# One transfer in place of two for q and k of a pair of heads, with eight tokens in sequence on a partition

## The chip, the cores and the metric

The kernel runs on one core of a Trainium2 chip. The metric is the time of the whole program on the device, in microseconds (us); lower is better.

## The reference, cut to what matters

Three blocks follow one another: an attention over 4 x 8 heads with 576 tokens of 64 values each, a two-layer expert block, and a second block whose two first products are multiplied with each other. The change lies in the loading of the attention's q and k:

```python
Sd = S // factor                      # factor = 4, S = 576
q_d = q.reshape(B, H, Sd, factor, D).mean(axis=3)
k_d = k.reshape(B, H, Sd, factor, D).mean(axis=3)
...
out_d = sm_attn(q_d, k_d, v_d)        # attention among the 144 group means
out_up = np.repeat(out_d, factor, axis=2)
mask = np.abs(pos[:, None] - pos[None, :]) < factor
...                                   # attention within the band |i - j| < 4
return (out_up + out_local).astype(np.float32)
...
h = x @ w_in
g = h * (1.0 / (1.0 + np.exp(-1.702 * h)))
x = g @ w_out
a = x @ w1
b = x @ w2
h = a * b @ w3
out = h @ w_out2
```

All of it is float32. The kernel splits each operand of a large product into a high and a low part and adds three matmuls (`mm3`, lines 118 to 120).

## The kernel before, in words

Heads are worked on in 16 pairs, numbered n = 4 b + hp: four pairs for each of the four batches b. A pair fills 128 partitions after its transposition: 64 values of one head, 64 of the other.

For a pair, `att_load` fetches q and k into the tiles s_q and s_k, one buffer each, and v into s_v. `t_piece` ("T") turns q and k over, so that the 64 values of each head lie on partitions and the 576 tokens along the free dimension (qT, kT, with 144 groups u of 4 tokens r), and adds up the tokens of each group (qd, kd). `s_local` and `s_pool` ("S") form the scores, `p_piece` ("P") transposes the exponentials, `v_pool` and `v_local` ("V") multiply them with v and store x_d.

Pairs 0 to 7 (the first two batches; `PE_T = 2`) are turned over by TensorE: the tile has 72 partitions, each holds 2 times 4 tokens of both heads, and each of two pieces c = 0 and 1 makes four 72 x 128 transposes into a PSUM tile ps_t (line 284), which ScalarE then writes out in group order (line 285). Pairs 8 to 15 take another branch (lines 243 and 280), with 32 x 32 transposes on VectorE.

The transfers of pairs 0 to 7 are issued in line 250, two for q and two for k: on the SyncE queue for pair 0, on ScalarE's own queue for pairs 1 to 7. ScalarE carries these issues out in its own order of instructions, between its activations. Pair n + 2 is loaded in the first `p_piece` of pair n, when pair n + 1 has been turned over; pair 5 is loaded in `s_pool` of pair 4; pair 1 before the loop over the w34 steps.

The pieces of batch 0 are put one by one between the matmuls of the first stage (the product w3 w_out2, tiles ps_w, w3t, w34s), those of later batches between the matmuls of `h_step` and `y_step` for the batch before. The weights come packed in 64-bit words and are decoded on the way: a transfer into `st`, ScalarE's `size_of` (line 166), VectorE's three steps (lines 173, 176, 179), and `split` (lines 114 and 115). Staging tiles come from pools of two and three buffers.

The Tile framework's scheduler makes the order of instructions on every engine when the program is built. It works with priorities and with times that it estimates itself for each instruction and transfer, and gives out buffers in that order. The trace shows this order: pieces of the source stand apart or between one another.

Of the kernel before, what the change touches and what calls it, by code (L numbers as in the profile page):

```python
# [8 lines left out]
F32 = mybir.dt.float32  # L9
# [3 lines left out]
AF = mybir.ActivationFunctionType  # L13
# [7 lines left out]
def fused_kernel(ctx, tc, q, k, v, w_in, w_out1, w1, w2, w3, w_out2, out):  # L21
    nc = tc.nc
    B, H, S, D = q.shape
    FAC = 4
# [9 lines left out]
    UC = SD // 2  # L34
# [37 lines left out]
    att = att_end.enter_context(tc.tile_pool(name="att", bufs=1))  # L72
# [11 lines left out]
    ident = const.tile([128, 128], F32, name="ident")  # L84
# [144 lines left out]
    def head_ap(src, b, hp, tok, dims):  # L229
        off = ((b * H + 2 * hp) * S + tok) * D  # L230
        return bass.AP(src.tensor, src.offset + off, dims)

    def att_load(n, names="qkv", queue=None):
        b, hp = divmod(n, HP)
        queue = queue or nc.scalar
        for name, src in (("q", q), ("k", k)):
            if name not in names:
                continue
            if b >= PE_T:

                st = att.tile([128, S // 32, 32], F32, tag="s" + name, name="s_" + name)
                for i in range(4):
                    nc.sync.dma_start(out=st[i * 32:(i + 1) * 32], in_=bass.AP(
                        src.tensor, src.offset + (b * H + 2 * hp + i // 2) * S * D + i % 2 * 32,
                        [[D, 32], [32 * D, S // 32], [1, 32]]))
                at["s" + name, n] = st
                continue
            st = att.tile([UC, 2, FAC, 2, D], F32, tag="s" + name, name="s_" + name)
            for c in range(2):
                queue.dma_start(out=st[:, c], in_=head_ap(  # L250
                    src, b, hp, c * UC * FAC, [[FAC * D, UC], [D, FAC], [S * D, 2], [1, D]]))
            at["s" + name, n] = st
        if "v" not in names:
            return
        st = att.tile([UC, 2, 2, FAC * D], F32, tag="sv", name="s_v")
        queue.dma_start(out=st, in_=head_ap(
            v, b, hp, 0, [[FAC * D, UC], [S * D, 2], [UC * FAC * D, 2], [1, FAC * D]]))
        at["sv", n] = st
# [15 lines left out]
    def t_piece(n, name, c):  # L274
        if c == 0:
            at[name, n] = att.tile([128, SD, FAC], F32, tag=name + "T", name=name + "T")
        st, dst = at["s" + name, n], at[name, n]
        if n // HP >= PE_T:
            if c == 0:
                nc.vector.transpose(dst.rearrange("p u r -> p (u r)"), st.rearrange("p a b -> p (a b)"))  # L280
        else:
            ps = pst.tile([128, FAC, UC], F32, tag="t", name="ps_t")
            for r in range(FAC):
                nc.tensor.transpose(ps[:, r], st[:, c, r].rearrange("p h d -> p (h d)"), ident[:UC, :UC])
            nc.scalar.activation(dst[:, c * UC:(c + 1) * UC].rearrange("p u r -> p r u"), ps, AF.Copy)
        if c == 1:
            if name == "q":
                d = qd[:, :SD]
            else:
                d = at["kd", n] = att.tile([128, SD], F32, tag="kd", name="kd")  # L290
            if n // HP in QK_V:
                nc.vector.tensor_reduce(d, dst, op=ALU.add, axis=X)
            else:
                nc.gpsimd.tensor_tensor(d, dst[:, :, 0], dst[:, :, 1], op=ALU.add)
                for r in range(2, FAC):
                    nc.gpsimd.tensor_tensor(d, d, dst[:, :, r], op=ALU.add)

    def v_means(n):
        sv = at.pop(("sv", n))
        nc.gpsimd.tensor_tensor(  # L300
            sv[:, :, :, :2 * D], sv[:, :, :, :2 * D], sv[:, :, :, 2 * D:], op=ALU.add)
        vd = at["vd", n] = att.tile([UC, 2, 2, D], F32, tag="vd", name="vd")
        nc.gpsimd.tensor_tensor(vd, sv[:, :, :, :D], sv[:, :, :, D:2 * D], op=ALU.add)
        if n + 1 < B * HP:
            att_load(n + 1, "v")
# [35 lines left out]
    def s_pool(n, own_exp):  # L341
        if n % HP == 0 and n > 0:
            att_load(n + 1, "qk")
# [39 lines left out]
    def p_piece(n, i0, i1):  # L383
        if i0 % NPH == 0 and i0 // NPH >= (n in LOCAL):
            at["PT", n, i0 // NPH] = att.tile(
                [KW, min(NPH, NPT - i0), 128], F32, tag=f"PT{i0 // NPH}", name="PT")
        i0 = i0 if n not in LOCAL else max(i0, NQB)
        ps = pst.tile([KW, i1 - i0, 128], F32, tag="t", name="ps_pt")
        for i in range(i0, i1):
            if i < NQB:  # L390
                src = at["el", n][:, i]
            else:
                kc, j = divmod(i - NQB, NPB)
                src = at["ep", n][:, j, kc * UC:(kc + 1) * UC]
            nc.tensor.transpose(ps[:, i - i0], src, ident)  # L395
        nc.scalar.activation(at["PT", n, i0 // NPH][:, i0 % NPH:i0 % NPH + i1 - i0], ps, AF.Copy)
        first = i0 == (0 if n not in LOCAL else NQB)
        if first:
            v_means(n)
            if n % HP < HP - 1 and n + 2 < B * HP:  # L400
                att_load(n + 2, "qk")
# [110 lines left out]
    def stage(n, what, own_exp):  # L512
        if what == "T":
            return [lambda name=name, c=c: t_piece(n, name, c) for name in "qk" for c in range(2)]
        if n in LOCAL and what in "SPV":
            if what == "S":
                return [lambda: s_pool(n, False)]
            if what == "P":
                return [lambda: p_piece(n, NPH, NPH + 4), lambda: p_piece(n, NPH + 4, NPT)]
            return [lambda: v_pool(n), lambda: l_out(n, 0, HQ), lambda: l_out(n, HQ, NQB)]  # L520
        if what == "S":
            return [lambda: s_local(n, 0, HQ, own_exp), lambda: s_local(n, HQ, NQB, own_exp), lambda: s_pool(n, own_exp)]
        if what == "P":
            return [lambda i=i: p_piece(n, i, min(i + 4, NPT)) for i in range(0, NPT, 4)]
        return [lambda: v_pool(n), lambda: v_local(n, 0, HQ), lambda: v_local(n, HQ, NQB)]
# [460 lines left out]
```

## Time and profile before

| | |
|---|---|
| Time, median of 3 runs | 893.88 us (893.79 to 894.19) |
| The profiled execution | 894.5 us, of which its span from first to last instruction is 892.7 us |
| TensorE, matmuls | 846.7 us busy (95% of the span) |
| VectorE (DVE) | 602.2 us (67%) |
| ScalarE (ACT) | 388.0 us (43%) |
| GpSimd (POOL) | 146.0 us (16%) |
| Mean granted TensorE clock | 0.988 of full speed |

Busy time doesn't count DMA issues: an engine that issues a transfer looks idle in it. The queues that issue are shown with a q (ACTq, SPq). PEld is TensorE's loading of weights, which overlaps its matmuls.

### The profile page before, as it was taken

The numbers are of one execution on the slowest core, as the hardware profiler recorded it, in microseconds if no ns is written. First come the engines' busy times: TensorE is split into PE (matmuls) and PEld (weight loads), VectorE is DVE, ScalarE is ACT, GpSimd is POOL, SyncE is SP. The second block draws the span as 40 slices with busy tenths as digits, with TensorE's granted clock in tenths as the row PEclk, the third lists the DMA queues.
The fourth block names the chain that finished last, engine by engine and source line by source line (L and its number), as shares of the span: only waits on it lengthen the run. The fifth ranks groups of instructions, "written<-read, shape, count | busy, mean of one in ns | idle before, by whom it ended". The sixth has DMA issues, their size and how long they took to land.

```text
span 892.7 us, 13582 instructions
## 1 busy us (share of the span) xinstructions
PE 846.7 (95%) x5132; PEld 711.7 (80%) x5132; DVE 602.2 (67%) x1061; ACT 388.0 (43%) x750; POOL 146.0 (16%) x153
## 2 busy tenths in 40 slices
PE   5689979889999999999999999999999999999998
PEld 4567757666777777777789988889999899989996
DVE  5997597889999999747658784343556455555551
ACT  4667566567756344455336564342112211232111
POOL 7525241233232322301200000000000000000000
PEclk9799999999999999999999999999999999999999
DMA  8866574566665341543247889302556364645521
GB/s 231 271 207 164 154 234 145 155 164 179 152 188 111 78 128 43 162 98 70 64 137 277 322 305 366 130 1 68 226 186 262 107 247 165 250 140 217 196 83 71
DMA packets 140598, 150.76 MB, mean 169 GB/s; under 512 B 86898, under 2 KB 121460, under 8 KB 136436
## 3 DMA queue, kind: packets, MB, share of 16 engines
q1 hardware_dynamic: 119424, 141.21, 49.0%
q10 hardware_dynamic: 21108, 8.69, 4.3%
q8 instruction: 40, 0.66, 0.3%
q14 instruction: 26, 0.21, 0.1%
HBM read 117.75 MB, written 32.11 MB: 168 GB/s over the span
## 4 chain that ended last, share of the span: by engine, by line
PE 57%; DVE 3%; issue 1%; ACT 1%; DMA 0%; DVEq 0%; ACTq 0%
PE ps_ab L120 7%; PE ps_ab L118 7%; PE ps_ab L119 7%; PE ps_y L118 4%; PE ps_y L119 4%; PE ps_y L120 4%; PE ps_h L118 4%; PE ps_h L119 4%; PE ps_h L120 4%; PE ps_o L119 4%; PE ps_o L120 4%; PE ps_o L118 4%; DVE prod L484 1%; PE ps_pt L395 0%; DVE ql L487 0%
## 5 line engine op out<-in xcount | busy, mean ns | idle before, releaser
L118 PE MATMUL ps_h<-x_t,w 128*128 128x512 f32 (+1 forms) x320 | 122.5, 385 | 3.0 <-DVE w L115 2.6
L118 PE MATMUL ps_y<-gh,w 128*128 128x512 f32 (+1 forms) x320 | 122.0, 382 | 0.7 <-ACT gh L114 0.7
L119 PE MATMUL ps_h<-x_t,w 128*128 128x512 f32 (+1 forms) x320 | 119.0, 372 | 0.6 <-DVE x_t L115 0.6
L119 PE MATMUL ps_y<-gl,w 128*128 128x512 f32 (+1 forms) x320 | 118.5, 370 | 1.0 <-DVE gl L115 1.0
L120 PE MATMUL ps_y<-gh,w 128*128 128x512 f32 (+1 forms) x320 | 118.8, 371 | 0.0
L120 PE MATMUL ps_h<-x_t,w 128*128 128x512 f32 (+1 forms) x320 | 118.6, 371 | 0.0
L120 PE MATMUL ps_ab<-b_t,a_in 128*128 128x384 f32 x336 | 112.5, 335 | 0.0
L118 PE MATMUL ps_ab<-b_t,a_in 128*128 128x384 f32 x336 | 112.5, 335 | 0.0
L119 PE MATMUL ps_ab<-b_t,a_in 128*128 128x384 f32 x336 | 112.4, 334 | 0.0
L115 DVE TENSOR_TENSOR gl<-g_t,gh 128x512 fp32r<-128x512 f32 (+1 forms) x80 | 56.3, 706 | 55.6 <-ACT gh L114 55.1
L624 ACT ACTIVATE g_t<-ps_h 128x512 f32<-128x512 f32 (+1 forms) x80 | 44.1, 552 | 103.7 <-PE ps_h L120 102.6
L118 PEld LDWEIGHTS ps_h<-x_t,w 128*128 128x128 f32 x320 | 60.3, 189 | 17.1 <-DVE w L115 4.4
L114 ACT ACTIVATE abh<-ab 128x384 fp32r<-128x384 f32 x24 | 12.6, 526 | 137.5 <-DVE ab L749 137.5
L118 PEld LDWEIGHTS ps_y<-gh,w 128*128 128x128 f32 x320 | 60.3, 189 | 12.5 <-issue 2.2
L119 PEld LDWEIGHTS ps_h<-x_t,w 128*128 128x128 f32 x320 | 60.7, 190 | 10.5 <-DVE x_t L115 1.6
L120 PEld LDWEIGHTS ps_h<-x_t,w 128*128 128x128 f32 x320 | 60.5, 189 | 10.4 <-issue 0.2
L120 PEld LDWEIGHTS ps_y<-gh,w 128*128 128x128 f32 x320 | 60.3, 189 | 10.3
L119 PEld LDWEIGHTS ps_y<-gl,w 128*128 128x128 f32 x320 | 60.4, 189 | 10.1 <-DVE gl L115 1.3
L179 DVE SCALAR_TENSOR_TENSOR dec<-dec,st 128x512 int32<-128x512 int32 x72 | 61.3, 863 | 7.4 <-ACT dec L166 6.6
L118 PEld LDWEIGHTS ps_ab<-b_t,a_in 128*128 128x128 f32 x336 | 63.1, 188 | 0.9
L119 PEld LDWEIGHTS ps_ab<-b_t,a_in 128*128 128x128 f32 x336 | 63.1, 188 | 0.9
L120 PEld LDWEIGHTS ps_ab<-b_t,a_in 128*128 128x128 f32 x336 | 63.1, 188 | 0.0
(149 smaller groups left out, 1645.4 us busy)
## 6 DMA issues: line engine op xcount, KB each, us to landing
a_in<-a_d SPq DMA_DIRECT2D x24, 1792.0 KB
st<-in_moe_w_dram SPq DMA_DIRECT2D x32, 512.0 KB
a_d<-ap SPq DMA_DIRECT2D x8, 1792.0 KB
st<-in_moe_w_out_dram SPq DMA_DIRECT2D x24, 512.0 KB
st<-in_moe_w_in_dram SPq DMA_DIRECT2D x16, 512.0 KB
yr<-y_d SPq DMA_DIRECT2D x12, 384.0 KB
out_dram<-osb SPq DMA_DIRECT2D x17, 256.0 KB
s_v<-in_v_dram ACTq DMA_DIRECT2D x15, 288.0 KB
```

The source lines that it names most:

```text
L114: nc.scalar.activation(hi, raw, AF.Copy)
L115: lo_eng.tensor_tensor(lo, raw, f32(hi), op=ALU.subtract)
L118: nc.tensor.matmul(ps, ll, rh, start=start, stop=False, skip_group_check=more)
L119: nc.tensor.matmul(ps, lh, rl, start=False, stop=False, skip_group_check=more)
L120: nc.tensor.matmul(ps, lh, rh, start=False, stop=stop, skip_group_check=more)
L179: nc.vector.scalar_tensor_tensor(t, t, 3, st[:, :, 0], op0=ALU.logical_shift_left, op1=ALU.bitwise_or)
L484: (nc.vector if o in DVE_V else nc.gpsimd).tensor_tensor(t, at["vl", n][:, o:o + GT], s[:, o].unsqueeze(2).to_broadcast([128, GT, D]), op= ...
L624: nc.scalar.activation(g[:, :n], ps[:, :n], AF.Gelu_apprx_sigmoid)
```

## The change: what it does

`att_load` makes one transfer for q and one for k of a pair, where there were two each. Before, a partition held tokens 4u to 4u + 3 of the first half of the sequence and the same of the second half; now partition u holds tokens 8u to 8u + 7. The pieces c of `t_piece` still take four tokens of each partition, but these are now the groups 2u + c in place of 72c + u. So line 285 writes groups that lie two apart: neighbouring values in the order of its writing are 8 elements apart in qT and kT (32 bytes), where they were 4 apart (16 bytes). The sizes of tiles and the counts of transposes and activations stay.

```diff
-            st = att.tile([UC, 2, FAC, 2, D], F32, tag="s" + name, name="s_" + name)
-            for c in range(2):
-                queue.dma_start(out=st[:, c], in_=head_ap(
-                    src, b, hp, c * UC * FAC, [[FAC * D, UC], [D, FAC], [S * D, 2], [1, D]]))
+            st = att.tile([UC, 2 * FAC, 2, D], F32, tag="s" + name, name="s_" + name)
+            queue.dma_start(out=st, in_=head_ap(
+                src, b, hp, 0, [[2 * FAC * D, UC], [D, 2 * FAC], [S * D, 2], [1, D]]))
...
-                nc.tensor.transpose(ps[:, r], st[:, c, r].rearrange("p h d -> p (h d)"), ident[:UC, :UC])
-            nc.scalar.activation(dst[:, c * UC:(c + 1) * UC].rearrange("p u r -> p r u"), ps, AF.Copy)
+                nc.tensor.transpose(ps[:, r], st[:, c * FAC + r].rearrange("p h d -> p (h d)"), ident[:UC, :UC])
+            nc.scalar.activation(
+                dst.rearrange("p (u c) r -> p c r u", c=2)[:, c], ps, AF.Copy)
```

## Rows read from the trace of the kernel before

**Rows 1.** Busy time by stretch: us, PE, PEld, DVE, ACT, POOL, PEclk, DMA share, GB/s.

```profile
0.00:223.00 223.00, 185.28 (x1349) 140.74 (x1350) 177.78 (x294) 139.65 (x309) 87.89 (x108) 0.95 0.66 190
223.00:893.00 670.00, 661.43 (x3784) 570.94 (x3783) 424.37 (x768) 248.38 (x443) 58.09 (x46) 1.00 0.50 162
20.00:80.00 60.00, 47.31 (x344) 35.48 (x342) 57.82 (x94) 37.11 (x102) 28.09 (x27) 0.89 0.70 215
```

**Rows 2.** Waits of TensorE, 0 to 223 us: total us, times, longest.

```profile
PE ps_w L573 <- DVE dec L179: 17.1, 5, 9.1
...
PE ps_sp L352 <- POOL kd L296: 3.5, 1, 3.5
...
PE ps_pt L395 <- ACT kT L285: 2.5, 2, 1.7
...
PE ps_pt L395 <- ACT PT L396: 1.8, 2, 1.3
```

**Rows 3.** Issues of transfers by tile and line: ns min/median/max, first and last start.

```profile
L250 ACTq DMA_DIRECT2D s_q<-in_q_dram x14: 805/807/1424, 11.2 to 190.7; - x14
L250 SPq DMA_DIRECT2D s_q<-in_q_dram x2: 792/882/971, 1.7 to 2.7; - x2
...
L243 SPq DMA_DIRECT2D s_q<-in_q_dram x32: 311/446/1356, 216.3 to 418.3; - x32
...
L256 ACTq DMA_DIRECT2D s_v<-in_v_dram x15: 307/308/365, 34.9 to 421.4; - x15
```

**Rows 4.** ScalarE's groups by form: count, busy us, mean ns, idle before.

```profile
L739 ACT ACTIVATE u_t<-ps_ab 128x384 f32<-128x384 f32 x24 | 11.8, 492 | 20.5 <-PE ps_ab L120 20.5
L285 ACT ACTIVATE qT<-ps_t 128x288 f32<-128x288 f32 x16 | 10.3, 711 | 5.6 <-PE ps_t L284 5.6
L413 ACT ACTIVATE od<-ps_vp 128x144 f32<-128x144 f32 x16 | 4.5, 283 | 6.6 <-PE ps_vp L410 4.6 <-DVE xo L507 1.9
```

**Rows 5.** VectorE's reductions by form; line 471 reads every ninth element.

```profile
L337 DVE TENSOR_REDUCE mx<-el 128x5 f32<-128x360 f32 x12 | 6.3, 521 | 0.0
L337 DVE TENSOR_REDUCE mx<-el 128x4 f32<-128x288 f32 x12 | 5.3, 440 | 0.0
...
L471 DVE TENSOR_REDUCE r<-s 128x9 f32<-128x63 f32 x4 | 1.1, 264 | 0.1
```

**Rows 6.** Waits of ScalarE, 0 to 223 us: the one put to these loads.

```profile
ACT PT L396 <- DMA s_k<-in_k_dram: 8.1, 4, 2.9
```

**Rows 7.** Timeline around two groups of issues: start, us, then the instruction.

```profile
43.43 1.65 ACTq L250 DMA_DIRECT2D s_k<-in_k_dram  x2
...
45.13 0.60 ACT L396 ACTIVATE PT<-ps_pt 72x512 f32<-72x512 f32 x1 [2.87 <-DMA s_k<-in_k_dram]
...
46.96 0.66 PE L573 MATMUL ps_w<-ident,dec 128*128 128x128 f32 x4 [0.82 <-DVE dec L179]
...
54.07 0.63 PE L573 MATMUL ps_w<-ident,dec 128*128 128x128 f32 x4 [2.23 <-DVE dec L179]
...
71.29 1.89 ACTq L250 DMA_DIRECT2D s_k<-in_k_dram  x2
...
73.88 0.52 PE L395 MATMUL ps_pt<-ident,ep 128*72 128x128 f32 x3 [0.52 <-ACT PT L396]
```

**Rows 8.** Timeline: issues for pair 0 and pair 5, and pair 5's first transposes.

```profile
3.51 2.42 SPq L250 DMA_DIRECT2D s_k<-in_k_dram  x2
...
130.53 0.81 ACTq L250 DMA_DIRECT2D s_q<-in_q_dram  x1
...
137.12 0.41 PE L284 MATMUL ps_t<-ident,s_q 72*128 72x72 f32 x4
```

**Rows 9.** Stretches of 5 us, columns as in the first group.

```profile
40.00:45.00 5.00, 3.94 (x14) 2.91 (x15) 5.00 (x5) 0.60 (x1) 4.81 (x5) 0.66 0.63 187
...
55.00:60.00 5.00, 5.00 (x54) 4.04 (x51) 4.81 (x8) 2.15 (x5) 1.66 (x2) 0.68 0.85 288
...
85.00:90.00 5.00, 3.97 (x36) 3.03 (x35) 1.73 (x3) 2.40 (x5) 2.67 (x4) 1.00 0.80 215
```

## The prediction, made before the result was known

> **What bounds the kernel now.** I read the busy time by stretch first. TensorE works 661.4 of the last 670 us, so nothing that the change touches can win there; pairs 8 to 15 take their own branch and stay as they are. Up to 223 us, where pairs 0 to 7 are loaded and turned over, TensorE works 185.3 us and stands idle for 37.7 us [rows 1]. A gain or a loss can only come out of these 37.7 us. Next the waits of TensorE in that stretch: 17.1 us end with VectorE's last decoding step in line 179, 9.1 us of them once, before the first weights are there; waits that ScalarE ends are 2.5 us for kT and 1.8 us for PT, and 3.5 us is for GpSimd's sum kd, which stands behind kT [rows 2]. Between 20 and 80 us VectorE is the fullest engine: 57.8 of 60 us [rows 1]. What ScalarE saves there reaches TensorE only as far as VectorE can follow.
>
> **What is removed: half of the issues.** The old transfers number 32: 28 on ScalarE's queue and 4 on SyncE's. An issue on ScalarE takes 0.805 us at 72 partitions with 8 rows of 256 bytes each [rows 3]. After it there are 14 on ScalarE and 2 on SyncE with 16 rows per partition. Rows of 256 bytes stay rows of 256 bytes, because the two heads still lie interleaved in the tile; bytes and rows per pair stay the same (2 x 1,152 rows), so I count no time of the DMA engines as won or lost.
>
> What one larger issue takes isn't in the trace. The nearest rows: v, with 4 rows of 1 KB on each of 72 partitions, 0.307 us; pairs 8 to 15, with 18 rows of 128 bytes on 32 partitions, 0.311 us at the least; q, with 8 rows, 0.805 us [rows 3]. The second has as many rows as q in all (576), so the number of rows alone doesn't explain 0.805. If what costs is the four-level pattern, the issue stays at 0.805 us, and ScalarE gets back 14 x 0.805 = 11.3 us. If it grows with the rows of a partition, the slope from v to q is (0.805 - 0.307) / 4 = 0.125 us a row, 16 rows take 1.80 us, and against 2 x 0.805 = 1.61 us this loses 14 x 0.19 = 2.7 us. I take 1.2 us, in the middle, since the rows point both ways: 14 x (1.61 - 1.2) = 5.7 us of ScalarE's time.
>
> **How much of that is on the path?** An issue that stands between two activations hides behind the one still running. Where two or four stand in a row ScalarE waits: 8.1 us in four places are put to the issues for s_k [rows 6]. I followed the two where TensorE waits soon after. From 41.7 to 45.1 us all four issues of pair 2 run; PT is copied only at 45.13, after 2.87 us, decoding comes behind it, and TensorE waits 0.82 us at 46.96. But the next wait for line 179, 2.23 us at 54.07 [rows 7], stands behind a VectorE without a gap, which then simply waits longer: I count 0 there, at most 0.8. At 71.29 us the two issues for s_k hold back PT, and TensorE waits 0.52 us at 73.88 [rows 7]. One issue in place of two shortens 1.61 to 1.2 us, thus takes some 0.4 us off it. In the other two places TensorE has matmuls at hand: 0. Sum: -0.4 us; with a flat 0.805 us and both places in full 0.8 + 0.5 = -1.3 us; with 1.80 us some +0.2 us.
>
> **SyncE at the start.** The two issues for k last until 5.93 us [rows 8]; the loads of weights behind them in SyncE's queue come up to 2 us earlier if an issue stays flat. The first two weight tiles were issued ahead, and the first wait of 9.1 us is for these. I count 0.
>
> **Waiting for a whole transfer.** The first piece now needs all 8 tokens of a partition. The tightest case before is pair 5: the second issue for q starts at 130.53 us and ends at 131.34, the first transpose comes at 137.12 [rows 8], 5.8 us later and without a wait. The new transfer is issued in the first one's place, sooner than that. I count 0; work that covers it are the matmuls in between. With that cover gone it would cost the difference of the landings, below 0.8 us (one issue) for a pair.
>
> **The other order of writing.** Line 285 writes 288 values per partition in 0.711 us. Activations with values side by side: 144 in 0.283 and 384 in 0.492 us, that is 0.871 ns a value, and 0.408 us for 288 [rows 4]. So the 16-byte step costs 0.30 us already. For 32 bytes there is no row of ScalarE. The nearest is a reduction on VectorE that reads 36 bytes apart: its neighbours give (521 - 440) / 72 = 1.125 ns a value and 116 ns beside, thus the 63 values take (264 - 116) / 63 = 2.35 ns each, 2.1 times as long [rows 5]; ScalarE's 16-byte step stands at 1.92 against 0.871 ns, 2.2 times. The wider step thus seems to cost nothing more: bounds 0 and another 0.30 us on each of 32 writes, 9.7 us of ScalarE. I take 0. The Trainium skill (SBUF — State Buffer, section Door 1: The DMA port swizzle) says that an access which goes on to a new 16-byte line pays. By that rule the 16-byte step pays for every value already and 32 bytes change nothing: 0 us by the rule, 0 by the row taken, and no run here shows the wider step.
>
> The Trainium skill (DMA: Bandwidth & Descriptors, section Rules for kernel authors) tells one to put small transfers together, as under 64 KB they are mostly overhead. These have 144 KB, and the trace shows no wait for their landing; by its 2.0 us for each transfer (same page, Anatomy of one DMA) 16 fewer would be an estimated 32 us, all beside other work.
>
> **The order made anew.** The scheduler makes the order from its own estimates, and 16 instructions fewer will shift pieces up to 223 us. How much this moves I bound from rows: in 40 to 45 and 55 to 60 us the granted clock is 0.66 and 0.68, that is, partly at the lower of two levels, 1.2 in place of 2.4 GHz. With TensorE at work throughout the second, such a stretch costs (1 - 0.68) x 5 = 1.6 us. A stretch with gaps, such as 85 to 90 us, leaves 1.0 us idle, and the next after it was granted less [rows 9]. So one such event more or less is worth 1.6 to 2.6 us, more than all that the issues give.
>
> **Rivals, each with its time.** My sum starts from the profiled execution, 894.5 us (892.7 of span and 1.8 around it), which is 0.6 above the median of 893.88; differences are applied to the median. A measurement tells 0.2%, 1.8 us, from no change.
> - No change that can be told (0.38): -0.4 us, rounded for the small chance of more to -0.6: 893.3 us. Its own range is 892.1 to 895.6.
> - ScalarE's freed time reaches TensorE (0.20): 0.8 + 0.5 us, and another 0.8 where VectorE's decoding at 54.07 moves up as well: -2.1, 891.8 us. For it speaks that line 179 ends most of TensorE's waits [rows 2], against it a full VectorE [rows 1]. It decides if an issue stays below 0.9 us and VectorE shows gaps at 45 us.
> - The new order loses or spares a stretch at the lower clock: faster by 1.6 and the 0.4, 891.9 us (0.16); slower by 1.6 + 1.0 us, 896.5 us (0.18). The slower one decides if one more idle time of about a microsecond falls between 25 and 150 us with a lower clock behind it.
> - The wider step costs (0.08): from 0.85 us for line 285. At 1.0 us kT is late twice (two activations each) in the waits of 2.5 us for kT and once in the 3.5 us for kd [rows 2]: 3 x 2 x 0.30 = 1.8, and 0.6 for the first pair: +2.4, 896.3 us.
> - That the change doesn't do what it says, at 1.61 us or more for an issue, gives 893.9 to 894.1 us and lies in the first case.
>
> Faster by over 0.2%: 0.20 + 0.16 = 0.36; within: 0.38; slower: 0.18 + 0.08 = 0.26. The range that leaves out no more than 2 in 10 runs from 890.2 (the faster cases with 1.6 us more) to 896.9 us.
>
> **What would show it.** In the trace after: issues of line 250, 14 on ScalarE, at about 1.2 us (0.8 or 1.8 at the bounds); line 285 at 0.71 us; the wait of ScalarE put to the loads of k at half of 8.1 us or less; idle time of TensorE up to 223 us at 37 us, with the same kinds of waits; after 223 us nothing. The prediction is wrong if that idle time moves by over 2 us, if the stretches at the lower clock are more or fewer, or if line 285 passes 0.85 us.

## The result, and the profile after

The changed kernel takes 905.49 us (median of 4 runs, 903.11 to 907.36) against 893.84 (891.24 to 894.19) of the kernel before: a ratio of 1.0136, with a 95% interval of 1.0099 to 1.0172. It is slower by 11.6 us. The profiled execution took 905.09 us, 903.3 of them its span. Lines behind the transfer stand one higher in this kernel: 249 for the transfer, 283 for the transposes, 284 for the write.

First the edits themselves. The issues of transfers of the changed kernel (columns as in [rows 3]) and the group of ScalarE that answers to line 285 in [rows 4]:

```profile
L249 ACTq DMA_DIRECT2D s_q<-in_q_dram x7: 807/829/1429, 11.1 to 195.5; - x7
L249 SPq DMA_DIRECT2D s_q<-in_q_dram x1: 976/976/976, 1.6 to 1.6; - x1
L249 ACTq DMA_DIRECT2D s_k<-in_k_dram x7: 807/807/830, 14.2 to 197.5; - x7
L249 SPq DMA_DIRECT2D s_k<-in_k_dram x1: 1722/1722/1722, 2.7 to 2.7; - x1
```

```profile
L284 ACT ACTIVATE qT<-ps_t 128x288 f32<-128x288 f32 x16 | 11.7, 758 | 9.2 <-PE ps_t L283 9.1
```

Half as many issues, and on ScalarE's queue each as short as before: 0.807 us with 16 rows to a partition as with 8. (On SyncE's queue the one issue for k took 1.722 us; the two for k took 2.42 us together [rows 8].) The write grew from 0.711 to 0.758 us. ScalarE's wait of 8.1 us put to the loads of k [rows 6] is gone. Each part of the edit thus costs little or gives something back, and still 11.6 us are lost. Busy time by stretch (columns as in [rows 1]):

```profile
0.00:223.00 223.00, 181.08 (x1315) 138.13 (x1315) 170.67 (x287) 136.38 (x300) 82.19 (x102) 0.92 0.65 186
223.00:893.00 670.00, 662.95 (x3793) 571.73 (x3792) 431.60 (x773) 255.12 (x451) 65.14 (x51) 1.00 0.50 162
```

Behind 223 us little changed; ahead of it TensorE worked 4.2 us less in the same time, at a granted clock of 0.92 in place of 0.95. Where the loss arises can be seen by milestones. At 84 us both kernels are in step: the fourth copy of w34s (line 586) begins at 84.00 us before and at 84.04 after. Pair 3's local scores (line 333) come at 101.30 and 104.30; the first product of y (`ps_y`) begins at 140.37 us before and at 150.85 after, and the first u_t of the second block (line 739) at 615.94 and 626.55. So the loss, 10.5 us, arises between 84 and 151 us and is only carried on behind that. The waits of TensorE from 84 to 156 us, of the kernel before and then of the changed one (us in total, times, longest):

```profile
PE ps_sp L352 <- POOL kd L296: 3.5, 1, 3.5
PE ps_t L284 <- DVE xo L426: 1.7, 1, 1.7
PE ps_pt L395 <- POOL el L375: 1.2, 1, 1.2
PE ps_h L119 <- DVE x_t L115: 0.6, 1, 0.6
```

```profile
PE ps_h L118 <- ACT x_t L114: 4.8, 1, 4.8
PE ps_pt L395 <- POOL el L375: 4.3, 1, 4.3
PE ps_t L283 <- DVE xo L426: 2.5, 1, 2.5
PE ps_h L119 <- DVE x_t L115: 2.2, 1, 2.2
PE ps_sp L352 <- DVE el L336: 0.3, 1, 0.3
```

In sum these are 7.0 us before and 14.1 after, 7.1 more. The clock adds to it. Stretches of 5 us of the changed kernel: us, TensorE's busy time, granted clock, DMA share, GB/s:

```profile
135.00:140.00 5.00, 0.64 (x1) 0.89 0.99 262
140.00:145.00 5.00, 2.80 (x10) 0.50 0.85 256
145.00:150.00 5.00, 4.71 (x61) 0.92 0.70 247
```

After 4.4 us of idle time TensorE goes on at a granted clock of 0.50, the lower of its two levels (1.2 in place of 2.4 GHz); in the next stretch, where it works 4.71 of 5 us, it is granted 0.92. Over 84 to 156 us the mean granted clock is 0.95 before and 0.88 after. On TensorE's 57.6 us of work there that is about 57.6 x (1 - 0.88 / 0.95) = 4.2 us, an estimate from these two rows (before, then after; columns as in the last ones), though the two stretches don't hold quite the same work; 7.1 + 4.2 = 11.3 us stand against 10.5 seen.

```profile
84.00:156.00 72.00, 64.34 (x472) 0.95 0.63 183
84.00:156.00 72.00, 57.60 (x434) 0.88 0.61 175
```

None of the five waits is for the loads of q and k or for line 284, which were changed. What stands ahead of them is seen in the timeline of the changed kernel around batch 0's last pair (pair 3), the lines that matter of each engine:

```profile
114.19 0.43 DVE L173 TENSOR_SCALAR st<-st 128x512 int32<-128x512 int32 x1 [1.88 <-DMA st<-in_moe_w_out_dram]
...
117.00 0.43 DVE L173 TENSOR_SCALAR st<-st 128x512 int32<-128x512 int32 x1 [0.84 <-DMA st<-in_moe_w_in_dram]
...
118.02 0.22 DVE L372 RECIPROCAL sm<-sm 128x12 f32<-128x12 f32 x1
...
118.12 1.78 POOL L300 TENSOR_TENSOR s_v<-s_v 72x512 f32<-72x512 f32 x1 [7.66 <-DMA s_v<-in_v_dram]
119.86 1.72 POOL L375 TENSOR_TENSOR el<-el,sm 128x648 f32<-128x648 f32 x1
...
121.64 1.75 PE L395 MATMUL ps_pt<-ident,el 128*72 128x128 f32 x8 [4.32 <-POOL el L375]
...
139.36 0.79 PE L118 MATMUL ps_h<-x_t,w 128*128 128x512 f32 x1 [4.81 <-ACT x_t L114]
142.36 0.79 PE L119 MATMUL ps_h<-x_t,w 128*128 128x512 f32 x1 [2.20 <-DVE x_t L115]
...
144.79 1.80 PE L333 MATMUL ps_s<-kT,qT 64*64 64x72 f32 x36
...
150.85 0.39 PE L118 MATMUL ps_y<-gh,w 128*128 128x512 f32 x1
```

And of the kernel before:

```profile
107.55 0.43 DVE L173 TENSOR_SCALAR st<-st 128x512 int32<-128x512 int32 x1 [0.54 <-DMA st<-in_moe_w_in_dram]
...
110.45 0.43 DVE L173 TENSOR_SCALAR st<-st 128x512 int32<-128x512 int32 x1 [1.20 <-DMA st<-in_moe_w_out_dram]
...
112.47 0.22 DVE L372 RECIPROCAL sm<-sm 128x12 f32<-128x12 f32 x1
...
112.84 1.27 POOL L375 TENSOR_TENSOR el<-el,sm 128x648 f32<-128x648 f32 x1 [5.36 <-DVE sm L372]
112.89 1.51 DVE L173 TENSOR_SCALAR st<-st 128x512 int32<-128x512 int32 x1
...
115.12 1.73 POOL L300 TENSOR_TENSOR s_v<-s_v 72x512 f32<-72x512 f32 x1
...
128.12 1.54 PE L333 MATMUL ps_s<-kT,qT 64*64 64x72 f32 x36
...
140.37 0.39 PE L118 MATMUL ps_y<-gh,w 128*128 128x512 f32 x1
```

What can be seen here are exchanges of places. Before, GpSimd scales the scores (line 375) and then adds up s_v for the next pair (line 300); after, the addition stands first and waits for its transfer. On VectorE two decode steps (line 173) that wait for weights stood ahead of the reciprocal (line 372) before too, with 0.54 and 1.20 us of waiting, and the next decode step behind it (112.89 us). After, one decode step more stands ahead of it, that at 117.00 us with 0.84 us of waiting. The reciprocal comes 5.5 us later, and 3.0 us of these it has from the later scores. On TensorE batch 1's first scores (line 333) stood in the gap ahead of the last x_t and now stand behind it. The edit touches none of these instructions.

### The profile page after: what moved, and what is told of

It is laid out like the page before. It is cut to its first block, busy times and chain, and to the rows that moved or that the text cites. A ratio compares the mean times of both kernels' runs of the same rounds, so it can differ in the third digit from the quotient of the medians.

```text
span 903.3 us, 13550 instructions
## 1 busy us (share of the span) xinstructions
PE 850.6 (94%) x5132; PEld 714.9 (79%) x5132; DVE 603.4 (67%) x1061; ACT 391.9 (43%) x752; POOL 147.3 (16%) x153
## 4 chain that ended last, share of the span: by engine, by line
PE 57%; DVE 3%; DMA 0%; issue 0%; ACT 0%; DVEq 0%; ACTq 0%
PE ps_ab L120 6%; PE ps_ab L118 6%; PE ps_ab L119 6%; PE ps_y L118 5%; PE ps_y L119 4%; PE ps_y L120 4%; PE ps_h L118 4%; PE ps_h L120 4%; PE ps_h L119 4%; PE ps_o L120 4%; PE ps_o L119 4%; PE ps_o L118 4%; DVE prod L484 1%; PE ps_pt L395 0%; DVE ql L487 0%; PE ps_sp L352 0%
## 5 line engine op out<-in xcount | busy, mean ns | idle before, releaser
L120 PEld LDWEIGHTS ps_h<-x_t,w 128*128 128x128 f32 x320 | 60.8, 190 | 10.5 <-issue 0.5
L120 PEld LDWEIGHTS ps_y<-gh,w 128*128 128x128 f32 x320 | 60.5, 189 | 10.6 <-issue 0.6
L173 DVE TENSOR_SCALAR st<-st 128x512 int32<-128x512 int32 x72 | 39.8, 554 | 35.0 <-DMA st<-in_moe_w_out_dram 19.0
```

Of the source, the lines that this page charges most:

```text
L120: nc.tensor.matmul(ps, lh, rh, start=False, stop=stop, skip_group_check=more)
L173: nc.vector.tensor_scalar(low, low, 29, None, op0=ALU.logical_shift_right)
```

## The experiments

The theory: the scheduler laid the program out anew, and that order, not the transfers, costs the time. Its rival: the larger transfer or the wider write costs it, directly or by what lands later. To tell them apart the order of one program was imposed on the code of another, by a dependency without a semaphore from each instruction to the next on its engine, for all five engines. "Moved" below means an edit of such a list, with the changed kernel's code. All ratios are against the kernel before, run beside each program, with the 95% interval; gains in us are differences of medians.

### The order apart from the code

```diff
 # the changed kernel's code, and at its end:
+    for engine, at in ORDER_OF_BEFORE.items():
+        for a, b in zip(at, at[1:]):
+            tc.add_manual_dep(made[engine][b], made[engine][a].name, NoSync)
```

> The changed kernel, with ordering edges (no waits) that put every instruction of every engine in the order of the kernel before; each single transfer stands where the first of its two stood. Theory 'order' (the 11.6 us come from the order that the scheduler made anew, not from the transfers or the writes): the time is back at the kernel before, 891 to 895 us, ratio 0.997 to 1.001, TensorE idle for about 37 us up to 223 us. Theory 'cost' (the larger transfer lands later or blocks others, or the wider write step holds up what follows): about 905 us in this order too, ratio 1.010 to 1.016.

Measured: 893.1 us, ratio 0.9999 (0.9979 to 1.002). With the whole edit in place and the old order of instructions the loss is gone, to 0.2%. The write still takes 0.766 us for qT there, the waits of TensorE from 84 to 156 us are 7.2 us, and up to 223 us it stands idle for 37.1 us (37.7 before).

The reverse, the code of before in the changed kernel's order (`ORDER_OF_AFTER`):

> The kernel before, its two transfers and its writes unchanged, with ordering edges that put every instruction in the order of the changed kernel; the second transfer of a pair is issued right behind the first. Theory 'order': 902 to 908 us, ratio 1.009 to 1.016, with TensorE's waits of 4 to 5 us near 121 and 139 us. Theory 'cost': 893 to 895 us, ratio 0.999 to 1.002.

Measured: 903.78 us, ratio 1.013 (1.0097 to 1.0164), the loss without the edit. Its waits in the same stretch, 12.4 us, are of the same kinds as the changed kernel's:

```profile
PE ps_h L118 <- ACT x_t L114: 3.7, 1, 3.7
PE ps_t L284 <- DVE xo L426: 3.3, 1, 3.3
PE ps_pt L395 <- POOL el L375: 2.9, 1, 2.9
PE ps_h L119 <- DVE x_t L115: 2.3, 1, 2.3
```

So the time goes with the order, whichever code it is given to. No run imposes on a code the order that it already has; but as either imposed order brings the time of the kernel that it was taken from, within the noise, the imposing itself isn't seen to cost anything.

Two more programs that the scheduler ordered for itself. The new layout with two transfers, of 36 partitions each:

```diff
-            queue.dma_start(out=st, in_=head_ap(
-                src, b, hp, 0, [[2 * FAC * D, UC], [D, 2 * FAC], [S * D, 2], [1, D]]))
+            for p0, p1 in ((0, UC // 2), (UC // 2, UC)):
+                queue.dma_start(out=st[p0:p1], in_=head_ap(
+                    src, b, hp, p0 * 2 * FAC, [[2 * FAC * D, p1 - p0], [D, 2 * FAC], [S * D, 2], [1, D]]))
```

> The changed kernel with each transfer cut into two of 36 partitions, so the layout and the writes are the new ones but the count of transfers is the old one; the scheduler makes an order of its own (neither of the two). Theory 'order': any time of a spread of several us around 893 to 907, not tied to the count of transfers; I guess 898 us, ratio 1.000 to 1.012. Theory 'cost' by the size of the transfer: 893 to 895 us; by the writes: 905 us.

Measured: 912.18 us, ratio 1.0225 (1.0193 to 1.0257). It loses more, and elsewhere: its waits from 84 to 156 us are only 7.5 us, but pair 3's local scores (line 333) come at 109.44 us, against 101.30 before, and of the 17.6 us by which the first u_t is late (633.5 against 615.9) 10 arise behind the first product of y (147.9 against 140.4). This code was not run in an old order, so what its transfers cost of that and what its order costs is not told apart. Its issues for 36 partitions with 16 rows:

```profile
L250 ACTq DMA_DIRECT2D s_q<-in_q_dram x14: 794/796/1413, 14.2 to 201.9; - x14
```

And the code of before with one number of the scheduler's priorities changed, and no instruction:

```diff
-    early = {"st": 0, "dec": 0, "pri": 200}
+    early = {"st": 0, "dec": 0, "pri": 190}
```

> The kernel before with one priority of the scheduler (that of the decoding in the first stage) at 190 in place of 200: the same instructions and transfers, some 280 rows of TensorE's order stand elsewhere. Theory 'order': the time moves by 1 to 6 us either way although nothing that is computed or moved is changed, ratio off 1 by 0.001 to 0.007. Theory 'cost': nothing, ratio 0.999 to 1.001.

Measured: 898.91 us, ratio 1.008 (1.0049 to 1.0112). The loss lies in another place than the changed kernel's: the first product of y begins at 138.2 us, earlier than before, and the first u_t at 620.2, 4.3 us later; between 140 and 260 us TensorE's waits for w of line 115 are 7.5 us, against 2.6 before. So the three programs that the scheduler ordered anew (the changed kernel, halves and this one) are all slower than the one before, by 0.8 to 2.3%.

### Which places in the order

All of these are the changed kernel in its own order, with a few instructions moved. (In two expectations below, the xo written at 90 us is called pair 2's; by its buffers it is pair 1's, and that at 111.83 and 115.14 pair 2's. The moves are as described.) Whether a move gained anything is judged against the changed kernel's own ratio, 1.0136 (1.0099 to 1.0172): with the half-widths of both intervals added in squares, a difference is clear from about 0.0045 on, that is 4 us.

```diff
 GpSimd, order of issue                      # el_ahead_of_v
-  L300 s_v
   L375 el, L377 ep      (pair 3)
+  L300 s_v
 VectorE                                     # sm_early_el_ahead: this too
+  L371 sm, L372 sm, L426 xo
   L173 st (114.19 us) ... L173 st (117.00 us)
-  L371 sm, L372 sm, L426 xo
```

> The changed kernel with its own order of instructions held fixed, and one swap on GpSimd: pair 3's scaling of the near and far scores (lines 375 and 377) stands ahead of the addition on s_v (line 300) that waits for the next v transfer, not behind it. If the whole late part of batch 0's last pair hangs on the chain of single places, the scaling starts when VectorE's reciprocal is done (118.24 us in the changed kernel's profile), not at 119.86: 1.6 us earlier, about 903.9 us. If the 11.6 us come from many small places all over the order, or from the transfers, the time stays at 905.5 within 0.5 us.

> The same swap on GpSimd, and on VectorE pair 3's lines 371, 372 and the second write of xo (line 426) moved ahead of the two decode steps (line 173, at 114.19 and 117.00 us) that wait for weight transfers. Chain of single places: the scores' exponentials end at 113.4 us, so the scaling can start at about 113.9 in place of 119.86, and the time falls by about 6 us, to 899.5 (the first TensorE transposes of line 395 at about 115.7, not 121.64). Many small places: 0 to 1 us of gain, since the next wait in the same chain takes the place.

Measured: 902.97 us, ratio 1.0107 (1.008 to 1.0135), and 901.8 us, ratio 1.0099 (1.0069 to 1.0128). By the medians the first gave 2.5 us in place of 1.6, the second 3.7 in place of 6; neither is clear of the noise. In the trace of the second the scaling does start 8 us earlier, and the transposes behind it don't wait. But the end gains only half of that: TensorE still waits 2.4 and 1.9 us for x_t, its waits for xo are 4.2 us in place of 2.5, and one of 1.9 us for gl (line 115) is new.

```profile
111.85 1.27 POOL L375 TENSOR_TENSOR el<-el,sm 128x648 f32<-128x648 f32 x1 [3.61 <-ACT dec L166]
```

Two tries ahead of that, where the loss begins:

```diff
 VectorE                                     # xo_early; with the two above: three_places
+  L426 xo, L426 xo
   L173 st, L176 st      (88.47 us)
-  L426 xo, L426 xo
 ScalarE and SyncE                           # four_places: three_places and this
+  L586 w34s / L587 w_d<-w34s
   L313 el x9 / L142 st, L149 st
-  L586 w34s / L587 w_d<-w34s
```

> The changed kernel in its own order, and on VectorE alone the two writes of pair 2's xo (line 426, at 90.00 and 90.65 us) moved ahead of the decode step (line 173) that waits for a weight transfer until 88.47. Chain of single places: both PSUM tiles come free at about 86.5, pair 3's q transposes start at about 88.0 in place of 90.55, and 2.5 us of the loss go if nothing behind takes it up: 903.0 us. Since the scaling of pair 3 also waits at 118.12 for a v transfer that this does not move, the rival within this theory is no gain here: 905.5 us.

> The three moves together. Chain of single places: 2.5 and 6 us add up to about 8.5 of the 11.6 us, so 897 us. If the moves are not independent, the 6 us alone: 899.5. Many small places: over 903.

> The kernel of three_places with a fourth place set back: ScalarE's third copy of w34s (line 586) and SyncE's store of it (line 587) stand ahead of pair 2's nine exponentials (line 313) and of the two weight transfers (lines 142 and 149), not behind them. In three_places VectorE's write of xo (line 426) waited 4.34 us until 89.86 for that store, because xo and w34s share a ring of buffers, so moving xo on VectorE alone gave nothing. Chain of single places: xo is written at about 86, the first q transposes of pair 3 run at about 86.5 in place of 90.41, the local scores of pair 3 (line 333) at about 101.5 in place of 104.29, and the time falls by 2 to 3 us, to 896.5. Many small places: 898.5 to 899.5 as before the move.

Measured: xo_early 905.82 us, ratio 1.0125 (1.0089 to 1.0161), no gain; three_places 898.98, 1.007 (1.0046 to 1.0094); four_places 900.4, 1.0077 (1.0049 to 1.0106), not the 896.5 expected. Both of the latter are clear of the changed kernel, but not of one another. In three_places the write of xo did not come earlier, it only waited for something else:

```profile
89.86 0.49 DVE L426 TENSOR_TENSOR xo<-ps_v,od 128x320 f32<-128x320 f32 x1 [4.34 <-DMA w_d<-w34s]
90.79 0.42 DVE L426 TENSOR_TENSOR xo<-ps_v,od 128x256 f32<-128x256 f32 x1 [0.44 <-DMA vw<-in_v_dram]
```

With w34s moved as well, the first xo is written at 85.34 us and four of the q transposes run at 87.17, as expected; but the second xo then waits 3.47 us, until 89.30, which the profile puts to a transfer of v, and pair 3's scores come at 102.94 in place of the 101.5 expected. The gain of 1.4 us there can't be told in the time.

To see where the rest lies, two hybrids. All engines follow one order up to the local scores of pair 3 (line 333) and the other behind them:

```diff
-order[engine] = new[engine]
+head = old[engine][:cut[engine]]            # old_then_new; new_then_old the other way
+order[engine] = head + [i for i in new[engine] if i not in head]
```

> The changed kernel's code; every engine issues in the order of the kernel before up to the local scores of batch 0's last pair (line 333, at about 98 us in that order), and all that is left in the changed kernel's order. If the loss arises place by place along the chain, as the milestones of the two profiles say (3.0 us late at these scores, 10.5 at the first ys), the part behind the cut costs 7 to 8 us: 901. If the first part's delay is what costs all, and the second part only hands it on: 894. If the parts multiply each other: over 904 here and in the other hybrid.

> The other way round: the changed kernel's order up to the same scores (104.30 us in its profile), and behind them the order of the kernel before. Place by place: 3 to 4 us of the 11.6, so 897. First part decides: 905. Part behind decides alone, the delay of the first being absorbed by waits for weight transfers: 893.8.

Measured: 907.25 us, ratio 1.0168 (1.0147 to 1.019), and 896.28 us, ratio 1.0035 (1.0011 to 1.006). The order ahead of the cut costs 0.35%, some 3 us, when that of before follows; the trace doesn't show where, as the first product of y begins at 140.73 us there, 0.4 later than before. The changed order behind the cut costs all of the loss (1.0168 can't be told from 1.0136), so the two don't simply add. But in old_then_new the seam adds a wait that neither order has (the first line), beside the known ones, so its loss is not the changed order's alone:

```profile
PE ps_sp L352 <- DVE el L336: 6.2, 1, 6.2
PE ps_h L118 <- ACT x_t L114: 4.5, 1, 4.5
```

Last, the two idle times of TensorE at 134 to 142 us:

```diff
 VectorE                                     # x_t_early
+  L115 x_t              (141.26 us)
   L173 st               (140.55 us)
-  L115 x_t
 TensorE and ScalarE                         # scores_in_wait
+  L333 ps_s / L284 kT
   L118 to L120 ps_h, six products / L586 w34s x2, L114 x_t
-  L333 ps_s / L284 kT
```

> The changed kernel in its own order, and one VectorE instruction moved: the second part of the last x_t of block 0 (line 115, at 141.26 us) stands ahead of the decode step (line 173, at 140.55) that waited 5.37 us for a weight transfer. TensorE's line 119 waited 2.20 us for that part. Place by place: 1.5 to 2.2 us of gain, 903.5. If the first product of that x_t (line 118, 4.81 us of waiting for ScalarE's part) and not this decides, or the weight transfer stops TensorE a little later anyway: 905.5.

> The changed kernel in its own order, and batch 1's first local scores (line 333, 1.80 us) moved on TensorE ahead of the six products that wait for the last x_t (lines 118 to 120 at 139.36), where the order of before has them; for that, ScalarE's second kT copy (line 284, at 139.22) goes ahead of its copies of w34s and x_t. Place by place: TensorE does them in its 4.81 us of idle time, 1.8 to 2.5 us of gain, 903.3. If the chain through x_t alone decides: 905.5.

> The moves of sm_early_el_ahead (GpSimd scaling ahead of the s_v addition, VectorE's lines 371, 372 and 426 ahead of two decode steps), of x_t_early and of scores_in_wait together, all behind the local scores of batch 0's last pair. Place by place: 3.7 us measured there and 3.5 to 4.5 more, so 897 to 898. If the moves take the same time from one another: 901.

> Those of five_moves and the moves of four_places ahead of these scores (xo, w34s and its store). Place by place, with the 3.3 us that the reverse hybrid put on the part ahead of the cut: 895 to 896.5. If the part ahead of the cut is absorbed: as five_moves.

Measured: x_t_early 901.43 us, ratio 1.0083 (1.0059 to 1.0108), 4 us of gain in place of 2, and clear; scores_in_wait 902.97, 1.0102 (1.0077 to 1.0127), 2.5 us by the medians, as expected, but not clear; five_moves 902.58, 1.0098 (1.0074 to 1.0122), not the 897 to 898 of a sum and no better than x_t_early alone; all_moves 899.24, 1.0068 (1.0044 to 1.0092), not the 895 to 896.5 expected. The moves do not add: by the median, half of the loss is still there with all of them together. Waits of TensorE from 84 to 156 us in all_moves, 9.7 us, at a mean granted clock of still 0.88:

```profile
PE ps_t L283 <- DVE xo L426: 4.0, 3, 1.8
PE ps_h L118 <- ACT x_t L114: 2.1, 1, 2.1
PE ps_sp L352 <- DVE el L336: 2.0, 1, 2.0
PE ps_s L333 <- ACT kT L284: 1.1, 1, 1.1
```

Of the first two, 4.0 and 2.1 us, the old order has 0.7 us and none; what holds them in this order was not taken apart further. The trace is that of the fastest execution of all_moves (895.18 us; the others reach up to 903.96). In it the first product of y is 4.2 us late, but the first u_t only 0.7; where the 6 us of the median lie it doesn't show.

One try to beat both kernels, in the order of before with the changed code:

```diff
 GpSimd                                      # old_order_kd_first
-  L300 s_v              (between the q sums of pair 4)
   L296 qd, L294 kd, L296 kd
+  L300 s_v
```

> The changed kernel's code in the order of the kernel before, and one GpSimd instruction moved: the addition on s_v (line 300, 124.20 us, 1.79 us) that stands inside the q sums of the first pair of batch 1 goes behind the kd sums (line 296). TensorE's pooled scores (line 352) waited 2.90 us for kd there. If places in the order are what sets the time, TensorE goes on 1.7 us earlier and the time is about 891.5, a little under both kernels. If the wait is taken up by the next one (the exponentials behind it, or a weight transfer), 893.2.

Measured: 892.62 us, ratio 1.0 (0.9978 to 1.0023). The wait of 2.90 us for kd went, 1.22 us for VectorE's line 337 came in its place, and the time can't be told from before.

## Why the prediction was wrong

It said 893.3 us (890.2 to 896.9) with no change as the likeliest case; 905.49 lies 8.6 us beyond the range.

- **The order made anew** is the step that failed. It was put as one event, a stretch at the lower clock more or less, worth 1.6 to 2.6 us, with faster and slower nearly even, and the slower rival ended at 896.5. The kind was right, idle time between 25 and 150 us with a lower clock behind it, and so was the prediction's own sign of being wrong: TensorE's idle time up to 223 us went from 37.7 to 41.9 us. The size was not: with the edit held fixed, the two orders lie 12.4 us apart (893.1 against 905.49), and in the code of before 10.6 us (893.14 against 903.78). The event was sized from two 5-us stretches, 55 to 60 and 85 to 90 us; that the stretch behind the latter was granted less is right (0.73), though no row shown had it. What came instead was several such events, one behind the other. VectorE's reciprocal waits behind one decode step more (0.84 us), GpSimd's scaling behind an addition of 1.78 us, and TensorE then waits 4.3, 4.8 and 2.2 us: 7.1 us more of waits in all, and about 4 us by the clock. The 4.3 us do hang on these places, as they are gone in sm_early_el_ahead. TensorE's idle time in sum, 37.7 us [rows 1], would have been a scale that holds such a move: the 7.1 us are a fifth of it.
- **The sign.** Faster by a new order got 0.16 and slower 0.18. Three programs ordered anew here were slower by 0.8, 1.4 and 2.3%. An even chance gives three of three once in eight times, so this speaks against it, but weakly.
- **The issues:** the lower bound was right (0.807 us, not the 1.2 taken). That made the sum -1.3 rather than -0.4 us if both places gave in full; in the old order the edit measures -0.01%, within 0.2%, which tells neither from nothing. That a sum built on 1.2 us still fits is no merit of it: less than 1.8 us couldn't be told.
- **ScalarE's freed time** did not reach TensorE. In the old order with the new code ScalarE's wait of 8.1 us is down to 2.1 (listed there under "issue"), but its wait for TensorE's transposes in line 395 grew from 16.3 to 20.3 us. The two waits of TensorE that were to fall, 0.82 and 0.52 us [rows 7], are now 1.06 us and, one group later, 0.41:

```profile
45.88 0.66 PE L573 MATMUL ps_w<-ident,dec 128*128 128x128 f32 x4 [1.06 <-DVE dec L179]
...
73.35 1.66 PE L333 MATMUL ps_s<-kT,qT 64*64 64x72 f32 x36 [0.41 <-ACT PT L396]
```

- **The write** of qT went from 0.711 to 0.758 us in the changed kernel; with the orders exchanged it takes 0.706 us with the old step and 0.766 with the new. That is 0.05 to 0.06 us, taken as 0 and bounded by 0.30. By the Trainium skill (SBUF — State Buffer, section Door 1: The DMA port swizzle) an access pays for each new 16-byte line, so by that rule a 32-byte step should cost no more than one of 16. The trace differs by these 0.05 us; it agrees in that the price of the step (0.30 us) doesn't double.
- **Waiting for a whole transfer, and SyncE at the start,** counted 0, held: none of TensorE's waits up to 223 us is for s_q or s_k, and its first wait for weights is 9.0 us (9.1 before [rows 2]).
- **Joined transfers:** the Trainium skill (DMA: Bandwidth & Descriptors, section Rules for kernel authors) tells one to join small transfers, as this change does. No run here contradicts it, and none shows a gain: held in the old order, 16 transfers fewer give nothing that can be measured, and nothing of the estimated 32 us is seen. The section of the Trainium skill's page that the prediction's 2.0 us for each transfer were taken from (Anatomy of one DMA) gives them for transfers issued by GpSimd; these were issued by ScalarE and SyncE.

What stays open: how the 11.6 us share out among all exchanges in the order. Shown is that the order carries them, that all but some 3 us of them need the changed order behind pair 3's local scores, that one swap on VectorE (x_t_early) gives about 4 us, and that all moves together give about half. The gains of 2.5 us from other single moves are not clear of the noise. The share of the clock is an estimate.

## What to carry to other kernels

When a scheduler makes the order, an edit has two effects: its own, and that of the new order, which here was far above any term of the sum. Measure them apart by imposing the old order on the new code, before judging the edit. When predicting, look in the trace for what is in line behind a wait for a transfer on each engine, and give the range the width of several exchanges there, not of one idle time. And if you can, let the scheduler order the unchanged code anew a few times, as before_pri190 did once: that shows how far the order alone moves the time, and which way.

## What the runs showed of the hardware

An issue on ScalarE's queue keeps its price for the same pattern when its rows double: 0.807 us for 72 partitions with 8 or with 16 rows of 256 bytes, 0.796 for 36 partitions with 16. For this pattern the price follows neither the rows to a partition nor the partitions. ScalarE's write at a 32-byte step took 0.04 to 0.06 us more for 288 values than at 16 bytes (qT 0.711 to 0.758 and kT 0.705 to 0.746 us from the kernel before to the changed one, qT 0.706 to 0.766 with the orders exchanged).
